# A new order of steps and a new deal of PSUM banks in a one-core attention and MLP kernel

## The chip, the core and the metric

The kernel runs on one core of a Trainium2 chip. The metric is the time of one execution on the device in microseconds (us), as a median of runs; lower is better.

## What is computed

```python
# q, k, v: 8 x 8 x 576 x 64 (batch, heads, sequence, head size); w_in 512 x 2048; w_out 2048 x 512
q_s = softmax(q, axis=-1)                    # over the 64 elements of a head
k_s = softmax(k, axis=2)                     # over the 576 places of the sequence
kv  = einsum('bhsd,bhse->bhde', k_s, v)      # 64 x 64 for each head
x   = einsum('bhsd,bhde->bhse', q_s, kv)     # back to 4608 tokens x 512
h   = x @ w_in
g   = h * tanh(softplus(h))                  # Mish
out = g @ w_out
```

Everything is float32.

## The kernel before

**Arithmetic.** Each large float32 product is made from three TensorE passes over numbers split in a high and a low part: high by high, high by low, low by high. `w_hi`, `x_hi`, `x_mix_hi`, `g_mix_hi` make high parts with a copy on ScalarE (ACT), and `w_lo`, `x_lo`, `x_mix_lo`, `g_mix_lo` make low parts with a subtraction on VectorE (DVE) or GpSimd (POOL). One pass is a matmul of 128 x 512.

**Stages.** A first block of tokens goes through the plain path: `h_part` (hidden layer, bank `ph`, line 629) and `out_part` (output, bank `po`, line 670). The other blocks go in pairs, k = 0 to 3, through a scheme that replaces eight block products by seven. `first_product(k, n, p)` (steps A, line 823) is product p, of 7, for the hidden piece n; it adds six matmuls into a bank `px`, `py` or `pz`. Products 1, 6, 5 and 3 of one piece add into the same bank `px`, and between them `partial` (steps C, line 859, ACT) copies the sum so far out of the bank; `joined` (J, line 863, DVE) and `g_mish_quad` (N, line 867, ACT) finish the piece. Then `g_mix` (GX), `g_mix_hi` (GH, line 889) and `g_mix_lo` (GK) prepare the Mish results, and `second_product(k, f, p)` (steps BB, line 839) multiplies them into banks `qx`, `qy`, `qz`. Each A or BB is six matmuls.

**Attention.** Heads come in pairs `e`. K (`a_kexp`, line 473) and Q are exponentiated on ACT; sums, maxima and transposes run on DVE, subtraction and scaling of Q on POOL. `a_kv2` (line 573, banks `pkv`, `pt`) makes the 64 x 64 matrices, `a_x2` (line 538, banks `px`, `pt`) applies them. The steps of attention for later blocks stand between the products of earlier ones.

**Weights.** `w_whole`, `w_mix` and `w_mix_out` build the weights of the seven products and write them to DRAM (`ws`). From there `w_fetch(e)` (steps F, line 807) brings them back in tiles of 512 KB, issued by POOL. Each tile serves two products. There are six slots:

```python
RING = ["w0", "w1", "xa0", "xa1", "xa2", "xa3"]
...
tag = {2: "w14", 3: "w15"}.get(e, RING[(e - LEAD) % 6])
...
nc.gpsimd.dma_start(dst, src)
```

So POOL can issue fetch e only when TensorE has read fetch e - 6 for the last time, and POOL takes its instructions one after another.

**Order.** The table `ORDER` lists 2,522 steps by name and number, and each engine's queue holds its instructions in that order. SyncE (SP) issues the other transfers in the same order: loads of K, Q and V, raw weights, stores of mixed weights and results. A second table, `BANKS`, gives one of TensorE's eight accumulation banks, a letter from a to h, to each of 282 uses, in the order in which they are asked for. A use waits until the use before it in the same bank has been read out. A planner outside the kernel wrote both tables; it isn't part of the program.

Of the kernel before, what the change touches and what calls it, by code (L numbers as in the profile page):

```python
# [9 lines left out]
F32 = mybir.dt.float32  # L10
# [27 lines left out]
Y10 RM27 ZT5 ZT4 RA27 G10 GL10 RB27 MQ7 RC27 SQ6 WM8.0p WM8.1p SQ7 WH8.0 RH26 Y9 GA9 WH8.1 RH27 RH25 H44 H45 H46 B6
H47 H48 WL8.1 WL8.0 KS6 GL9 RD22 WW9v R29 R28 LK8 ST5 WK1 WK10 WP8.0 WP8.1 WK3 WK9 RO25 RL28 RO26 WM9.0p WM9.1p RO27
Y11 GA11 RA28 EQ6 EK6 EQ7 RA29 RM29 MK8 GL11 RB28 RC28 RB29 Q6 QZ6 Q7 O8 H49 O9 H50 H51 H52 H56 H57 H53 H54 H55 H58  # L40
H59 O10 RH28 WH9.0 Y12 WH9.1 QZ7 WL9.0 RC29 WL9.1 WK11 WP9.0 WP9.1 RW30 KB8 RH29 GA12 Y13 GA13 Y14 GA14 KM8 WW10v GL12
GL13 GL14 QM7 RO28 QM6 WM10.0p WM10.1p KP6 XP4 UE8.0 RW31 WH10.0 WH10.1 S6 U8.0 O11 T7 O12 WL10.0 WL10.1 RB30 RC30
RB31 RC31 V8 WK4 WP10.0 WP10.1 LQ8 TC7 Z5 Z4 RH30 RD29 ZL5 ZL4 WW11v RD30 MQ8 T6 WM11.0p TC6 UE8.1 OP13.3 OP13.0 XP6
XT6 WM11.1p Z6 ZT7 Z7 ZT6 WH11.0 MS8 WH11.1 U8.1 ZL6 WL11.0 ZL7 WL11.1 MT8 SQ8 EQ8 LK10 WP11.0 ST7 WP11.1 LQ9 ST4 ST6
Q8 WW12v OP14.3 OP13.2 OP13.1 H60 H61 OP14.2 PK6 OP14.1 HM23 H62 H63 QW8 Y15 GM23 QV8 S8 MK10 MQ9 WM12.0p WM12.1p QM8
WH12.0 MS9 RH31 WH12.1 KB10 G15 GL15 WL12.0 MT9 KM10 WL12.1 T8 RO31 SQ9 UE10.1 EQ9 UE10.0 V10 WP12.0 WP12.1 LQ10 WW13v
Q9 QW9 U10.0 QV9 U10.1 MQ10 WM13.0p QM9 WM13.1p HM19 HM24 OP14.0 HM28 HM20 OP15.2 OP15.3 OP15.0 OP15.1 PA WH13.0 GM28
GM24 GM20 WH13.1 MS10 T9 WL13.0 EV0.0v WL13.1 WW14v MT10 PX8 PK8 SQ10 EV0.1s ZT9 Z8 ZT8 EQ10 LK12 WP13.0 WP13.1 LQ11
EV0.2v ZL8 S10 Q10 MK12 WM14.0p WM14.1p EV0.3s QW10 WH14.0 KB12 Z9 WH14.1 KM12 WL14.0 QV10 WL14.1 MQ11 UE12.1 MS11
QM10 V12 WP14.0 WP14.1 WK8 ST9 WW15v ZL9 MT11 T10 SQ11 EQ11 UE12.0 Q11 U12.0 U12.1 QW11 QV11 WM15.0p WM15.1p QM11 HM31  # L50
HM17 HM26 HM16 HM22 HM30 HM18 GM26 WH15.0 GM22 WH15.1 GM16 GM17 GM30 GM31 GH0.1.0 GM18 WL15.0 T11 WL15.1 WW0v LQ12
LK14 ST8 WP15.0 WP15.1 PX10 PK10 HM21 GM19 Z10 ZT10 Z11 WM0.0p MK14 ZL10 ZL11 MQ12 WM0.1p MS12 WH0.0 GH0.1.1 WH0.1
GM21 WL0.0 WL0.1 WW1v MT12 HM35 HM32 HM41 HM33 HM37 ST10 WK12 WP0.0 WP0.1 WK13 SQ12 WM1.0p WM1.1p ZT11 EQ12 WH1.0 GM37
GM32 GM33 WH1.1 KB14 GK0.1.1 WL1.0 WW6v Q12 WL1.1 S12 LQ13 WK14 WP1.0 WK6 WP1.1 WK15 WK7 MQ13 KM14 F4 WM6.0p WM6.1p
# [36 lines left out]
A1.7.3 BB1.3.1 PK22 PX22 BB1.4.1 BB1.5.1 A1.7.4 BB1.6.1 BB1.7.1 N1.6.2 N1.7.1 QW24 GH1.2.0 N1.3.2 GH1.2.1 GX1.3.0v
# [968 lines left out]
```

## Time and profile before

| | us |
|---|---|
| median of the runs | 788.44 |
| lowest of the runs | 788.32 |
| the profiled execution's own time | 787.31 |
| its span from first to last instruction | 785.5 |
| TensorE (PE) busy in the span | 773.4 |
| DVE, ACT, POOL busy | 560.6, 516.7, 298.3 |

The profiled execution's time is 1.8 us over its span, which is what lies before the first and behind the last instruction, and 1.1 us under the median. TensorE's granted clock is full in every stretch of the page. A matmul's listed duration, 0.39 us, holds its way through the pipeline, so consecutive ones overlap; their pace is read from their number in a stretch.

### The profile page before, as it was taken

The page shows a single profiled execution, that of the slowest core. Times are in us where ns is not written, and L with a number is a line of the kernel's source. Part 1 is how long each engine was busy: PE and PEld are TensorE (multiplying, and loading weights), DVE is VectorE, ACT ScalarE, POOL GpSimd, SP SyncE. Part 2 cuts the span into 40 slices and gives each one's busy share as a digit, 9 for nine tenths or more (in the row PEclk, how much of TensorE's full clock was granted, in tenths as well). Part 3 has the DMA queues.
Part 4 walks back from the last instruction along what each step waited for, and adds up shares of the span by engine and source line. Part 5 has one row for each costly group of instructions (what it writes and reads, how often), then busy time and mean ns, then how long its engine had stood idle before and what let it go on. Part 6 is the DMA issues. An engine that isn't in the chain of part 4 may idle for free.

```text
span 785.5 us, 12653 instructions
## 1 busy us (share of the span) xinstructions
PE 773.4 (98%) x4592; PEld 623.5 (79%) x4592; DVE 560.6 (71%) x877; ACT 516.7 (66%) x958; POOL 298.3 (38%) x378
## 2 busy tenths in 40 slices
PE   8999999999999999899999999999999999999997
PEld 7787768788877877687786878888878888888886
DVE  7999987765899999445799996235878722427863
ACT  7997867777887675588986765567736423635451
POOL 7898735544463444332332323133211121121111
PEclk9999999999999999999999999999999999999999
DMA  9996955678988878975775877668656684666575
GB/s 344 405 349 226 349 183 187 238 258 284 315 274 296 274 225 299 308 243 176 260 250 170 273 268 239 207 184 261 217 172 224 197 289 141 214 210 191 188 240 188
DMA packets 80717, 192.75 MB, mean 245 GB/s; under 512 B 16016, under 2 KB 28560, under 8 KB 80656
## 3 DMA queue, kind: packets, MB, share of 16 engines
q0 software_dynamic: 28800, 104.08, 41.5%
q1 hardware_dynamic: 51712, 87.74, 32.2%
q8 instruction: 36, 0.59, 0.3%
q14 instruction: 25, 0.20, 0.1%
q10 hardware_dynamic: 144, 0.13, 0.1%
HBM read 152.08 MB, written 39.85 MB: 244 GB/s over the span
## 4 chain that ended last, share of the span: by engine, by line
PE 75%; DVE 9%; ACT 8%; DMA 3%; issue 3%; POOL 1%; SPq 0%; DVEq 0%; ACTq 0%; POOLq 0%
PE qx L839 15%; PE px L823 14%; PE ph L629 10%; PE qz L839 10%; PE qy L839 9%; PE py L823 7%; PE pz L823 3%; PE px L538 2%; PE po L670 1%; PE pt L573 1%; DMA ws<-ws 1%; DVE gs L224 1%; DVE g L224 1%; DVE wa L269 1%; DVE w_out L726 1%
## 5 line engine op out<-in xcount | busy, mean ns | idle before, releaser
L807 POOL DMA_DIRECT2D ws<-ws x200 | 107.9, 542 | 348.7 <-PE qx L839 75.2
L224 DVE TENSOR_TENSOR gs<-g,gs 128x1024 fp32r<-128x1024 f32 x112 | 136.4, 1232 | 47.0 <-ACT gs L889 46.9
L889 ACT CAST gs<-g 128x1024 fp32r<-128x1024 f32 x112 | 116.5, 1051 | 76.2 <-PE qx L839 34.7
L839 PE MATMUL qx<-gs,ws 128*128 128x512 f32 x576 | 135.6, 391 | 0.0
L823 PE MATMUL px<-xh,ws 128*128 128x512 f32 x384 | 129.0, 391 | 2.3 <-DMA ws<-ws 2.0
L839 PEld LDWEIGHTS qx<-gs,ws 128*128 128x128 f32 x576 | 107.6, 188 | 26.3 <-issue 2.4
L629 PE MATMUL ph<-xs,wi 128*128 128x512 f32 x384 | 91.3, 392 | 0.6 <-DVE wc_out L276 0.5
L839 PE MATMUL qy<-gs,ws 128*128 128x512 f32 x384 | 90.9, 390 | 1.0 <-DVE gs L224 0.8
L839 PE MATMUL qz<-gs,ws 128*128 128x512 f32 x384 | 90.5, 390 | 0.0
L859 ACT COPY g<-px 128x512 f32<-128x512 f32 x72 | 41.5, 586 | 71.5 <-PE px L823 71.3
L823 PEld LDWEIGHTS px<-xh,ws 128*128 128x128 f32 x384 | 72.1, 188 | 19.3 <-issue 3.2
L839 PEld LDWEIGHTS qy<-gs,ws 128*128 128x128 f32 x384 | 71.8, 188 | 17.1 <-DVE gs L224 2.1
L629 PEld LDWEIGHTS ph<-xs,wi 128*128 128x128 f32 x384 | 71.4, 188 | 17.6 <-issue 2.0
L839 PEld LDWEIGHTS qz<-gs,ws 128*128 128x128 f32 x384 | 71.9, 188 | 16.5 <-issue 1.6
L224 DVE TENSOR_TENSOR g<-g,g 128x1024 f32<-128x1024 f32 x64 | 79.3, 1260 | 0.6
L823 PE MATMUL px<-xl,ws 128*128 128x512 f32 x192 | 74.7, 389 | 0.0
L863 DVE TENSOR_TENSOR g<-py,g 128x512 f32<-128x512 f32 x48 | 32.4, 683 | 57.7 <-PE py L823 29.6
L823 PE MATMUL py<-xh,ws 128*128 128x512 f32 x192 | 65.7, 390 | 0.0
L224 POOL TENSOR_TENSOR q<-q,qm 128x576 f32<-128x576 f32 (+1 forms) x31 | 41.2, 1328 | 31.9 <-DVE qm L383 18.6
L867 ACT ACTIVATE g<-g 128x512 f32<-128x512 f32 x72 | 43.2, 629 | 8.6 <-DVE g L863 8.3
L496 POOL TENSOR_TENSOR qe<-qe,qs 128x576 f32<-128x576 f32 x24 | 30.6, 1274 | 42.5 <-DVE qs L492 22.2
L629 PE MATMUL ph<-xs_odd,wi 128*128 128x512 f32 x192 | 44.9, 391 | 0.0
(169 smaller groups left out, 1287.9 us busy)
## 6 DMA issues: line engine op xcount, KB each, us to landing
ws<-ws POOLq DMA_DIRECT2D x197, 512.0 KB, 4.6
v<-in_v_dram SPq DMA_DIRECT2D x14, 594.0 KB, 5.8
ws<-m_out SPq DMA_DIRECT2D x32, 256.0 KB, 3.7
ws<-m_in SPq DMA_DIRECT2D x32, 256.0 KB, 3.5
raw_out<-in_w_dram SPq DMA_DIRECT2D x14, 512.0 KB, 7.7
kt_two<-in_kp_dram SPq DMA_DIRECT2D x12, 576.0 KB, 5.3
q<-in_qs_dram SPq DMA_DIRECT2D x24, 288.0 KB, 3.8
ws<-wi SPq DMA_DIRECT2D x24, 256.0 KB, 4.7
```

The lines of the kernel that those rows point to most:

```text
L224: eng.tensor_tensor(out, a, b, ALU.subtract)
L269: nc.vector.scalar_tensor_tensor(a, a, 3, low, ALU.logical_shift_left, ALU.bitwise_or)
L496: eng.tensor_tensor(q2, q2, z.unsqueeze(2).to_broadcast(list(q2.shape)), ALU.mult)
L538: nc.tensor.matmul((px, pt)[x][h][o], kvt[a, j], at[e + j]["qT"][x][a], start=True, stop=True)
L629: nc.tensor.matmul(gs[n], wi[f][:, a, t], x[:, z], start=t == 0 and i == 0, stop=t == HP - 1 and i == 2)
L807: nc.gpsimd.dma_start(dst, src)
L823: nc.tensor.matmul(dst, w[:, a, j], xc[k, p][z][:, j].rearrange("p b s -> p (b s)"), start=p in (1, 2, 7) and j == 0 and i == 0, stop=j == ...
L839: nc.tensor.matmul(psb[key, k][m], w[:, a, m], g[z][:, f % 2], start=first and i == 0, stop=f == NH - 1 and i == 2, skip_group_check=p in ...
L859: nc.scalar.copy(g_quad(k, n)[q], psb[1, k, n])
L863: nc.vector.tensor_tensor(g, psb[2 if q == 0 else 7, k, n], g, ALU.add)
L867: nc.scalar.activation(g, psb[1, k, n] if q == 1 else g, AF.Mish)
L889: nc.scalar.copy(t[0], gq[k, h][G_PART[p]])
```

## The change

The two tables are written anew by the planner. `ORDER` keeps its first 300 steps and holds the same 2,522 steps behind them in another sequence; `BANKS` keeps its first 70 letters. No function changes. The planner made the tables with two other settings: where POOL and DVE would take the port that they share at nearly the same moment, POOL is planned first; and a transfer is planned at 320 KB per us. No step changes its engine. Neither setting is in the program, which sees the order alone.

```diff
-RB16 RA18 RO14 RC16 RB15 RC15 H29 RH17 RA19 RM21 RH16 RH15 RA21 H30 H31 O5 RO17 RO16 RB19 RB18 RC19 RB21 RC18 RC21
...
+RB16 RA18 RO14 WK0 RB15 RM20 R31 RB18 RH17 RC16 RM21 QZ5 H29 RA19 RO17 RC15 H30 RH16 RB19 R26 RH15 H31 RC19 QM4 O5
...
 BANKS = """
...
-cfbhgebfdcefbgdh caefdfcebgbhcedb ghfdeacgbhgceaae aedfdfbaehfdabcg aefhfgbcbehdbagh dfcabgecfdhdecaf faafbggbfahbecdh
-gfcagbegdfehcdge fabfgchaedahahbf gdcechfgabdecfhe fbgeadbfhg
...
+hcgdfagdchbgeach gbedfaheahcgabdc ahebdhgfedacbfca bfhgbfdhgbfeddch adcecgfhcbadebea cgdhcdfbeaabghfe fefdceacbdeadbhg
+aefbdfgddhedbcfb dcfedcghabhbagef cdgbheagcfcfhbah eghefcdbhe
```

In the built program the number of matmuls, transfers and instructions of DVE and POOL is the same; ACT has 40 table loads in place of 46, because the order groups its functions differently. The engines leave the old order at about 57 us of the profiled execution (ACT and DVE), 59 us (POOL) and 67 us (PE).

**Place 1, the K and V product of pair 6** (`pkv6`, two banks; `po0` is the first block's output). On PE it follows one output step before:

```order
L670 MATMUL po0_0_610<-wo10_1001,gh10_1114 128x512 x2
L670 MATMUL po0_0_610<-wo10_1001,gl10_1116 128x512
L670 MATMUL po0_1_611<-wo10_1001,gh10_1114 128x512 x2
L670 MATMUL po0_1_611<-wo10_1001,gl10_1116 128x512
L670 MATMUL po0_2_612<-wo10_1001,gh10_1114 128x512 x2
L670 MATMUL po0_2_612<-wo10_1001,gl10_1116 128x512
L670 MATMUL po0_3_613<-wo10_1001,gh10_1114 128x512 x2
L670 MATMUL po0_3_613<-wo10_1001,gl10_1116 128x512
L573 MATMUL pkv6_1353<-v3_113,k6_1029 64x66
L573 MATMUL pkv6_1_1354<-v3_113,k6_1029 64x66
```

On DVE, the rows that end with the reading of bank `ph12`, which the second bank of `pkv6` takes over, were before (`gl` is a low part, `w_out` a whole weight):

```order
L726 TENSOR_TENSOR w_out2_1335<-wo2_668 128x512
L726 TENSOR_TENSOR w_out2_1335<-wo10_1001 128x512
L224 TENSOR_TENSOR gl12_1338<-ph12_1156,gh12_1326 128x512
L224 TENSOR_TENSOR gl13_1340<-ph13_1260,gh13_1329 128x512
L224 TENSOR_TENSOR gl14_1342<-ph14_1264,gh14_1332 128x512
```

On PE it now stands here, behind two groups of transposes (`pq6`, `pq7`) and another output step:

```order
L670 MATMUL po0_0_610<-wo12_1213,gh12_1265 128x512 x2
L670 MATMUL po0_0_610<-wo12_1213,gl12_1274 128x512
L670 MATMUL po0_1_611<-wo12_1213,gh12_1265 128x512 x2
L670 MATMUL po0_1_611<-wo12_1213,gl12_1274 128x512
L670 MATMUL po0_2_612<-wo12_1213,gh12_1265 128x512 x2
L670 MATMUL po0_2_612<-wo12_1213,gl12_1274 128x512
L670 MATMUL po0_3_613<-wo12_1213,gh12_1265 128x512 x2
L670 MATMUL po0_3_613<-wo12_1213,gl12_1274 128x512
L515 MATMUL pq7_1408<-ident_81,q7_1057 128x128 x4
L516 MATMUL pqt7_1409<-ident_81,q7_1057 128x128
L573 MATMUL pkv6_1415<-v3_113,k6_1090 64x66
L573 MATMUL pkv6_1_1416<-v3_113,k6_1090 64x66
```

On ACT, the rows from the end of the product `px4`, `px5` (just ahead of `pq6`) to the exponential `k6` that `pkv6` needs are now:

```order
L615 CAST xs_odd_1392<-px5_1358 128x512
L615 CAST xs_odd_1392<-px4_1357 128x512
L529 COPY qT6_1398<-pq6_1369 128x512
L530 COPY qTt6_1399<-pqt6_1370 128x64
L473 ACTIVATE k6_1090<-k6_1090 128x1152
```

The product moved behind later work, and its second bank is now one that `px5` had, no longer `ph12`.

**Place 2, fetch 170 of the weights** (k = 3; it takes the slot of fetch 164). On PE the twelve rows that end with its first reader were before, none of them reading `ws164`, whose last reader stands 21 rows above the first of them:

```order
L839 MATMUL qx3_0_7141<-gs3_1_0_6991,ws168_7065 128x512 x3
L839 MATMUL qx3_1_7142<-gs3_1_0_6991,ws168_7065 128x512 x3
L839 MATMUL qx3_0_7141<-gs3_1_0_6991,ws168_7065 128x512 x3
L839 MATMUL qx3_1_7142<-gs3_1_0_6991,ws168_7065 128x512 x3
L823 MATMUL px3_6_6951<-xh3_3_6524,ws167_7061 128x512
L823 MATMUL px3_6_6951<-xl3_3_6525,ws167_7061 128x512
L823 MATMUL px3_6_6951<-xh3_3_6524,ws167_7061 128x512 x2
L823 MATMUL px3_6_6951<-xl3_3_6525,ws167_7061 128x512
L823 MATMUL px3_6_6951<-xh3_3_6524,ws167_7061 128x512
L839 MATMUL qx3_0_7141<-gs3_1_1_6986,ws169_7063 128x512 x3
L839 MATMUL qx3_1_7142<-gs3_1_1_6986,ws169_7063 128x512 x3
L839 MATMUL qx3_0_7141<-gs3_1_1_6986,ws170_7129 128x512 x3
```

Now the row just ahead of the first of these is the last that reads `ws164`:

```order
L839 MATMUL qx3_0_7149<-gs3_1_0_7018,ws168_7097 128x512 x3
L839 MATMUL qx3_1_7150<-gs3_1_0_7018,ws168_7097 128x512 x3
L839 MATMUL qx3_0_7149<-gs3_1_0_7018,ws168_7097 128x512 x3
L839 MATMUL qx3_1_7150<-gs3_1_0_7018,ws168_7097 128x512 x3
L839 MATMUL qx3_0_7149<-gs3_1_1_6938,ws169_7078 128x512 x3
L839 MATMUL qx3_1_7150<-gs3_1_1_6938,ws169_7078 128x512 x3
L823 MATMUL py3_7_7112<-xh3_4_6645,ws171_7069 128x512
L823 MATMUL py3_7_7112<-xl3_4_6646,ws171_7069 128x512
L823 MATMUL py3_7_7112<-xh3_4_6645,ws171_7069 128x512 x2
L823 MATMUL py3_7_7112<-xl3_4_6646,ws171_7069 128x512
L823 MATMUL py3_7_7112<-xh3_4_6645,ws171_7069 128x512
L839 MATMUL qx3_0_7149<-gs3_1_1_6938,ws170_7158 128x512 x3
```

Between the last reader of the slot's old tile and the first reader of the new one stood 48 matmuls, and now 24. The same count for the 199 fetches that a matmul waits for, from the last matmul for which POOL must wait before it can issue the fetch (the reader of its own slot, or of one that stands ahead of it in POOL's queue) to the first that reads it: before, the smallest number was 30, eight times, and 26 fetches had 36; now three have 24, two 26 or 27, twelve 30, three about 32, and nineteen 36.

**Place 3, the bank `px3_0`** (k = 3, piece 0; `xh3_5` and `xh3_3` are the inputs of products 5 and 3). On PE the rows that end with the first matmul of product 3 were before, with product 5 further up:

```order
L823 MATMUL px3_1_6644<-xh3_5_6454,ws148_6688 128x512
L823 MATMUL py3_2_6754<-xh3_7_6513,ws148_6688 128x512
L823 MATMUL py3_2_6754<-xl3_7_6514,ws148_6688 128x512
L823 MATMUL py3_2_6754<-xh3_7_6513,ws148_6688 128x512 x2
L823 MATMUL py3_2_6754<-xl3_7_6514,ws148_6688 128x512
L823 MATMUL py3_2_6754<-xh3_7_6513,ws148_6688 128x512
L823 MATMUL py3_0_6613<-xh3_4_6734,ws146_6686 128x512
L823 MATMUL py3_0_6613<-xl3_4_6735,ws146_6686 128x512
L823 MATMUL py3_0_6613<-xh3_4_6734,ws146_6686 128x512 x2
L823 MATMUL py3_0_6613<-xl3_4_6735,ws146_6686 128x512
L823 MATMUL py3_0_6613<-xh3_4_6734,ws146_6686 128x512
L823 MATMUL px3_0_6584<-xh3_3_6524,ws146_6686 128x512
```

Now the first row is the last of product 5:

```order
L823 MATMUL px3_0_6624<-xh3_5_6512,ws144_6612 128x512
L823 MATMUL py3_2_6726<-xh3_7_6531,ws148_6679 128x512
L823 MATMUL py3_2_6726<-xl3_7_6532,ws148_6679 128x512
L823 MATMUL py3_2_6726<-xh3_7_6531,ws148_6679 128x512 x2
L823 MATMUL py3_2_6726<-xl3_7_6532,ws148_6679 128x512
L823 MATMUL py3_2_6726<-xh3_7_6531,ws148_6679 128x512
L823 MATMUL px3_0_6624<-xh3_3_6368,ws146_6681 128x512
```

One other product, six matmuls, now stands between the two that add into `px3_0`, where five stood before; the copy on ACT (line 859) has to fit in. In all, the places where a copy of line 859 or a Mish of line 867 has one product for it go from 11 to 24 between the start of k = 1 and the end, and two copies of line 767 join them.

## Rows read from the trace of the kernel before

**Rows 1.** The page: span, and busy time with share and instructions.

```profile
span 785.5 us, 12653 instructions
PE 773.4 (98%) x4592; PEld 623.5 (79%) x4592; DVE 560.6 (71%) x877; ACT 516.7 (66%) x958; POOL 298.3 (38%) x378
```

**Rows 2.** Windows, PE: length, busy us (instructions), granted clock, DMA share, GB/s.

```profile
55.00:140.00 85.00, 82.62 (x581) 1.00 0.71 238
140.00:300.00 160.00, 160.00 (x1123) 1.00 0.83 275
300.00:430.00 130.00, 126.45 (x702) 1.00 0.73 240
430.00:785.50 355.50, 351.54 (x1785) 1.00 0.68 216
```

**Rows 3.** Waits of PE: us in total, times, longest.

```profile
PE px L823 <- DMA ws<-ws: 2.0, 2, 1.3
...
PE pkv L573 <- DVE gl L224: 1.2, 1, 1.2
...
PE qy L839 <- DVE gs L224: 0.8, 1, 0.8
...
PE px L823 <- ACT g L859: 0.3, 1, 0.3
```

**Rows 4.** Windows, all engines (PE, PEld, DVE, ACT, POOL), one undisturbed stretch.

```profile
480.00:500.00 20.00, 20.00 (x90) 16.57 (x89) 7.38 (x17) 13.65 (x22) 6.09 (x9) 1.00 0.79 243
```

**Rows 5.** Line 807, the fetches: durations ns; time from issue to landing.

```profile
L807 POOL DMA_DIRECT2D ws<-ws x200: 527/535/753, 177.5 to 772.4; - x100
...
DMA to landing us min/median/max: 3.4/4.6/9.9
```

**Rows 6.** Timeline of POOL, 306 to 322 us: start, us, instruction.

```profile
314.59 0.57 POOL L807 DMA_DIRECT2D ws<-ws  x1
...
317.87 1.10 POOL L807 DMA_DIRECT2D ws<-ws  x2 [1.51 <-PE px L823]
```

**Rows 7.** Timeline of PE, 320 to 330 us.

```profile
322.22 0.47 PE L823 MATMUL px<-xh,ws 128*128 128x512 f32 x1 [0.66 <-DMA ws<-ws]
...
327.92 0.47 PE L823 MATMUL px<-xh,ws 128*128 128x512 f32 x1 [1.33 <-DMA ws<-ws]
```

**Rows 8.** Line 859, the copy out of a shared bank: ns min/median/max.

```profile
L859 ACT COPY g<-px x72: 565/589/631, 302.1 to 706.1; 128x512 f32<-128x512 f32 x72
```

**Rows 9.** Timeline of DVE, 97 to 103 us.

```profile
97.85 2.35 DVE L726 TENSOR_TENSOR w_out<-wo 128x512 f32<-128x512 f32 x2
100.12 1.87 DVE L224 TENSOR_TENSOR gl<-ph,gh 128x512 fp32r<-128x512 f32 x3
102.17 0.22 DVE L586 TENSOR_SCALAR rs<-pkv 128x1 f32<-128x1 f32 x2 [0.18 <-PE pkv L573]
```

**Rows 10.** Line 726, whole weights: ns min/median/max.

```profile
L726 DVE TENSOR_TENSOR w_out<-wo x16: 645/685/1784, 76.5 to 150.0; 128x512 f32<-128x512 f32 x16
```

**Rows 11.** ACT groups by line: count, busy us, mean ns, idle before.

```profile
L470 ACT ACT_TABLE_LOAD x12 | 15.4, 1283 | 2.9 <-DVE odd L510 2.2 <-DVE qTt L510 0.6
...
L529 ACT COPY qT<-pq 128x512 f32<-128x512 f32 x6 | 3.5, 589 | 3.1 <-PE pq L515 3.1
...
L473 ACT ACTIVATE k<-k 128x1152 f32<-128x1152 f32 x2 | 2.3, 1162 | 0.0
L615 ACT CAST xs_odd<-px 128x512 fp32r<-128x512 f32 x4 | 2.3, 592 | 1.8 <-PE px L538 1.0 <-DVE wc_out L276 0.8
...
L530 ACT COPY qTt<-pqt 128x64 f32<-128x64 f32 x4 | 0.9, 221 | 0.0
```

**Rows 12.** Timeline of PE, 104 to 112 us: transposes and an output step.

```profile
105.96 0.60 PE L515 MATMUL pq<-ident,q 128*128 128x128 f32 x4
...
106.42 0.70 PE L670 MATMUL po<-wo,gh 128*128 128x512 f32 x2
...
109.28 0.60 PE L515 MATMUL pq<-ident,q 128*128 128x128 f32 x4
```

More of the change, by code (lines that the diff above doesn't have):

```diff
@@ L38 @@
[L38 to L42, printed above, removed]
@@ new lines @@
+Q23 A1.7.5 GX1.1.1v F60 QW23 F58 QV23 A1.6.3 C1.7.3 MK26 BB1.0.1 MQ24 N1.0.3 J1.7.3 MS24 BB1.1.1 J1.4.2 N1.7.3
+GX1.0.1v N1.0.2 BB1.2.1 F62 GH1.2.0 QM23 A1.6.4 N1.6.1 N1.7.0 T23 N1.6.0 BB1.3.1 GX1.2.0v F61 GH1.1.3 J1.5.2 N1.6.3
+A1.7.3 MT24 GK1.1.3 PX22 N1.7.1 F64 F63 PK22 SQ24 BB1.4.1 GX1.3.0v EQ24 ZT23 KB26 LQ25 GK1.2.0 ST23 BB1.5.1 GH1.2.1
+V26 S24 XR23 BB1.6.1 J1.6.2 GK1.2.1 BB1.0.2 F66 N1.6.2 KM26 N1.4.2 MQ25 N1.5.2 A1.7.4 Q24 GX1.3.1v QW24 BB1.1.2 F65
+GH1.2.2 QV24 J1.7.2 QM24 BB1.7.1 N1.4.3 MS25 GK1.2.2 BB1.2.2 N1.7.2 GH1.2.3 MT25 GX1.2.1v BB1.3.2 GH1.7.0 F68 GK1.2.3
@@ new lines @@
+F67 BB1.4.2 GH1.7.1 GK1.7.0 BB1.5.2 F69 GX1.0.2v UE26.1 BB1.6.2 T24 DP1.0.0 GK1.7.1 GH1.7.2 BB1.0.7 F70 GX1.1.2v
+BB1.1.7 GX1.0.3v BB1.2.7 GH1.6.0 DP1.0.1 GK1.6.0 BB1.7.2 F72 GK1.7.2 BB1.3.7 GH1.7.3 F71 SQ25 DJ1.0.0 XR22 BB1.0.6
+DJ1.0.1 EQ25 GK1.7.3 DS1.0.1 GH1.6.1 BB1.4.7 Q25 ZT22 ST22 GX1.2.2v QW25 BB1.1.6 F73 DS1.0.0 LQ26 UE26.0 GK1.6.1
+BB1.5.7 QV25 BB1.6.7 QM25 GH1.6.2 T25 BB1.7.7 F74 U26.0 GX1.3.2v BB1.2.6 F75 GK1.6.2 GH1.6.3 PX24 F76 MQ26 BB1.3.6
+GX1.2.3v MS26 BB1.4.6 GH1.5.0 MT26 GK1.6.3 XR24 BB1.5.6 U26.1 SQ26 XR25 F77 BB1.6.6 GH1.5.1 GH1.3.0 GK1.5.1 BB1.7.6
@@ new lines @@
+EQ29 LQ30 Q29 A2.3.1 C2.2.0 J2.1.2 J2.0.2 A2.2.6 C2.3.0 A2.2.2 N2.0.2 C2.2.2 A2.3.6 F97 N2.1.3 MQ30 N2.0.1 F99 U30.0
+F100 A2.4.1 U30.1 A2.2.5 C2.4.0 N2.0.0 A2.4.2 C2.2.3 J2.2.3 A2.2.3 N2.2.3 F104 C2.3.2 A2.3.2 N2.2.1 QW29 A2.2.4 MS30
+A2.4.7 J2.2.2 F103 F101 MT30 J2.3.0 N2.2.2 A2.3.5 N2.1.0 J2.2.0 GH2.1.0 A2.3.7 N2.3.0 F105 GK2.1.0 C2.3.3 N2.2.0
+A2.4.6 QV29 F102 GH2.1.1 QM29 A2.3.3 T29 A2.5.1 J2.3.3 F106 SQ30 A2.5.7 EQ30 C2.4.2 LQ31 A2.3.4 C2.5.0 ST26 ST27
+A2.5.6 J2.3.2 F107 Q30 A2.4.5 C2.5.2 F109 A2.5.2 C2.4.3 J2.4.3 A2.4.3 J2.5.0 N2.3.1 GK2.1.1 N2.5.0 A2.4.4 QW30
@@ new lines @@
+GX2.1.0v N2.0.3 A2.6.2 N2.3.3 J2.4.0 N2.4.0 A2.6.1 GH2.1.2 A2.5.5 C2.6.0 F111 F108 J2.6.0 F110 A2.6.6 J2.4.2 C2.5.3
+GK2.1.2 A2.5.3 C2.6.2 MQ31 J2.5.3 MS31 A2.6.5 F113 N2.1.1 MT31 N2.6.0 A2.7.2 GX2.0.0v N2.5.1 QV30 PX28 F115 QM30 PK28
+XR29 XR28 A2.7.1 T30 ZT29 ZT28 ST28 S30 A2.6.7 C2.7.0 C2.6.3 J2.7.0 A2.7.6 J2.6.3 F112 XR32 GX2.0.1v ST29 A2.6.4
+C2.7.2 N2.6.3 A2.5.4 J2.6.2 A2.7.7 F114 SQ31 A2.7.5 XR33 F116 EQ31 DS1.2.1 DS1.2.0 Q31 BB2.0.1 C2.7.3 J2.7.3 BB2.1.1
+N2.7.0 GH2.1.3 A2.7.4 QW31 BB2.2.1 J2.7.2 N2.3.2 QV31 A2.6.3 J2.5.2 A2.7.3 N2.6.1 F117 N2.1.2 F118 GH2.2.0 F119
@@ L154 @@
+GK3.3.1 BB3.3.5 F193 BB3.2.3 GH3.3.2 GK3.3.2 BB3.4.5 BB3.5.5 F194 BB3.6.5 GH3.3.3 GK3.3.3 BB3.7.5 F195 GX3.1.3v
+BB3.3.3 DP3.1.1 DJ3.3.1 BB3.4.3 GX3.0.3v DS3.3.1 GH3.4.0 BB3.5.3 F197 GH3.4.1 GK3.4.0 BB3.6.3 DP3.1.0 GK3.4.1 BB3.7.3
+F198 DJ3.3.0 BB3.0.4 GH3.4.3 DJ3.1.0 DJ3.1.1 DS3.1.0 GH3.4.2 DS3.3.0 BB3.1.4 F199 DS3.1.1 F196 GK3.4.2 BB3.2.4 GK3.4.3
+BB3.3.4 BM3.4.4.0 BM3.5.4.0 BM3.6.4.0 BM3.7.4.0 BM3.4.4.1 DJ3.2.0 BM3.5.4.1 DS3.2.0 BM3.6.4.1 BM3.7.4.1 DK3.2.1.0
+DK3.2.1.1 DT3.2.1.0 DT3.2.1.1
 """
```

210 lines of the change are left out of this document (95 added, 115 removed).

## Prediction

> **What bounds the kernel now.** I read the page first. TensorE is busy for 773.4 of 785.5 us and no other engine is over 71% [rows 1], at a full granted clock in every stretch [rows 2]. So the question isn't which engine is slow on average, but where TensorE stands still, and whether it ever works below its own pace. The pace comes from an undisturbed stretch: 90 matmuls in 20.00 us [rows 4], 0.222 us for each pass of 128 x 512. With the number of matmuls unchanged, all that an order can change is idle time. The windows put it in place [rows 2]: 85.00 - 82.62 = 2.4 us between 55 and 140 us, none between 140 and 300, 130.00 - 126.45 = 3.5 us between 300 and 430, and 355.50 - 351.54 = 4.0 us behind 430. These last 4.0 are the tail, after the last matmul: joining and storing the last piece, which no order of the middle takes away. Idle time ahead of 55 us lies in the first 300 steps, which stay. So 2.4 + 3.5 = **5.9 us** is everything that the new order can remove. That makes a floor: 788.44 - 5.9 = 782.5 us, 0.75% under the median. A gain over 2%, which is about what a measurement of this kernel can tell from no change, would need 15.8 us and isn't there to be had.
>
> The waits of TensorE say what the 5.9 us are [rows 3]: 2.0 us in two waits for weight fetches, 1.2 us in one wait for DVE ahead of `pkv`, 0.8 us for a split of the Mish result on DVE, 0.3 us for a copy on ACT, and smaller ones. I go through them by kind, and ask for each what the new order puts in its place. The sum is made on the profiled execution; its differences are added to the median, which is 1.1 us above that execution's own time.
>
> **Waits for weight fetches, 2.0 us now.** A fetch takes 3.4 us at best, 4.6 at the median and 9.9 at worst from issue to landing [rows 5]. The two waits show what a slow one does. The fetch issued at 314.59 [rows 6] was used at 322.22 [rows 7], 7.6 us later, and TensorE stood for 0.66 us; the second of the pair issued from 317.87 on [rows 6] held it for 1.33 us at 327.92 [rows 7]. In the order these two had 30 and 36 matmuls between release and use, which is 6.7 and 8.0 us at 0.222 us each. So with 30 matmuls a median fetch has some 1.5 us to spare, and only a slow one is felt. The new order spends part of that margin (place 2): three fetches have 24 matmuls, 5.3 us; two have 26 or 27, 5.9 us; twelve have 30. The median fetch still lands in time for 24, by about 0.4 us if some 0.3 us pass between release and issue, an estimate. I price by the rate of before. One of eight fetches with 30 matmuls was slow, for 0.66 us: 0.08 us each, so twelve cost 1.0. One of 26 with 36 cost 1.33: 0.05 each, so the 22 with 32 or 36 cost 1.1. For 24 matmuls the same slow fetch, 7.6 + 0.3 us, would cost 2.6 us, for 26 or 27 some 2.0; at one in eight that is 0.32 and 0.25 each, 1.5 for the five. Sum **3.6 us in place of 2.0**. The bounds are 0, if all land at the median, and some 29 us if all twenty fetches under 33 matmuls land as late as the slow one (third rival).
>
> A page's rule speaks against a loss here. The rows have a median of 4.6 us for 512 KB [rows 5]. The Trainium skill, "DMA: Bandwidth & Descriptors", section on the anatomy of a DMA on the GpSimd path, has a fit of about 2.0 us plus the bytes over 436 GB/s, which by my working is 3.2 us for such a tile, below the fastest of the 200 rows; by it no fetch of either order would be late.
>
> **The pair-6 product, 1.2 us now.** Before, its second bank came from `ph12`, which DVE read late: two whole-weight additions took 2.35 us from 97.85, and the three low parts only began at 100.12 [rows 9]. In the new order (place 1) it needs the copies behind `px5` on ACT: two `xs_odd` at 592 ns, `qT` 589, `qTt` 221 and the exponential 1162 [rows 11], together 3.2 us. TensorE meanwhile has ten transposes and one output step: from 105.96 to 106.42 for five transposes, 106.42 to 109.28 for twelve passes [rows 12], 0.46 + 2.86 + 0.46 = 3.8 us. That covers the chain by 0.6 us, less handovers. I take 0.3 us, with bounds of 0 and 1.2. What is queued behind the waiting `pkv6` is all of TensorE. Its result then feeds `pt6` after one group of six matmuls, 1.3 us, through five small DVE instructions that stand behind a `w_out`. That addition takes 685 ns at the median and 1784 at most [rows 10]; I take 0.2 us more, with bounds of 0 and 1.5. The other 1.2 us of idle time between 55 and 140 us I leave as they are, with bounds of 0 and 3: this stretch keeps its crowd of weight conversions in another order, and I see no reason for either sign. So **2.4 becomes 1.7**.
>
> **Copies out of a shared bank, 0.3 us now.** Where product 5 and product 3 of a piece have one product between them (place 3), the copy of 589 ns [rows 8] must fit into six matmuls, 1.3 us. It does if ACT is free, with 0.7 us over; it fails if ACT is in a cast or a table load, 1283 ns [rows 11]. Before there were 11 such places, and one cost 0.3 us: 0.025 each. Now there are 26: **0.6 us**, from 0 to 5 if a table load stands in front of several.
>
> **The rest.** The waits for splits and the single small ones, 1.3 us, are kept at 1.3 (0 to 3): the chain from the last first products over Mish and splits to the second products has the same steps. Six table loads fewer, 6 x 1.283 = 7.7 us less on ACT [rows 11], are worth nothing on the path: ACT is idle for a third of the span [rows 1], and TensorE, which sets the end, hides it. SP and POOL hold the same transfers. POOL's Q steps now stand at other places between fetches, and since a fetch behind them waits, that is in the counts of place 2 only where a matmul is behind it.
>
> **Sum.** 3.6 + 1.7 + 0.6 + 1.3 = 7.2 us of idle time in place of 5.9, so 1.3 more: 788.44 + 1.3 = **789.7 us**, no change that a measurement would tell.
>
> **Rivals.** First, *the fetches land in time and their waits vanish*: 789.7 - 3.6 = 786.1 us, down to the floor of 782.5 if the other waits go too. For it: 4.6 us at the median fits even 24 matmuls [rows 5]; against it: before, two fetches with more room were late. The skill's DMA page would have it so. Chance 0.22. Second, *DVE becomes the bound between 55 and 140 us*: whole-weight additions stretch from 0.69 to 1.78 us at worst [rows 10] while POOL works beside them. If five or six more are stretched by 1.1 us, or an equal delay comes from the new order, in a part where DVE has no slack, TensorE waits for about 6 us more: 796 us. Chance 0.08. Third, the slow side: *the fetches become the bound from k = 1 on*. POOL issues in its order, so TensorE waits for each late tile. The price of a mean landing T on the twenty short ones is 20 T - 123.5 us: 3 (T + 0.3 - 5.3) and so on for each group. At the slow fetch's 7.6 us that is 29 us, 27 more than before: 815 us. It decides from about T = 7.1 us, where it takes 18 us; the median of 4.6 speaks against it, the 9.9 us of the worst for it. Chance 0.05. That the new order leaves TensorE's waits as they were gives 788.4 and falls under the forecast.
>
> **How the numbers follow.** The forecast has the remaining 0.65, spread over some 786 to 794 us. The range should leave out no more than 2 in 10: at its low end I take the floor, 782.5, since nothing below it can be had; at the high end the forecast with about half of the upper bounds (fetches 9, early part 4, copies 2, rest 2, 17 in all against 5.9) gives 799, and I stop at 798, so that the third rival is outside. Faster by over 2%: 0.01, a TensorE that ran faster than its own pace. Slower by over 2%: 0.05, the third rival. Within 2%: 0.94.
>
> **What would show it.** TensorE's busy time again near 773 us and 90 matmuls in 20 us. The wait ahead of `pkv6` at most a few tenths, for ACT or DVE and no longer for `gl`. Waits for `ws` in more places than two, mainly where k = 1 and 2 read the tiles with 24 matmuls, each under 2.6 us. The copies of line 859 named more than once. I'm wrong if idle time between 140 and 300 us, which is none now, appears, or if TensorE's idle time behind 55 us, tail apart, is over 16 us or under 2.

## The result, and the profile after

The changed kernel takes **781.8 us** at the median of its runs (781.06 to 782.77), against 788.76 for the kernel before: a ratio of 0.9914, with a 95% interval of 0.9895 to 0.9934. One of the four runs of before took 961.67 us; the ratio leaves it out, and without it the median of before is 788.44. The changed kernel is 0.9% faster, less than the 2% that I called the bound of a change, but clearly not none, and on the other side of 788.44 than my 789.7. It lies 0.7 us below the range's low end, which I had called a floor.

The page of the profiled execution after (its own time 782.30 us), which answers to [rows 1]:

```profile
span 780.5 us, 12662 instructions
...
PE 770.3 (99%) x4592; PEld 623.5 (80%) x4592; DVE 563.7 (72%) x877; ACT 511.0 (65%) x952; POOL 297.3 (38%) x378
```

The span is 5.0 us shorter. TensorE's *busy* time is 3.1 us shorter too, with the same 4592 instructions at a full granted clock. That was not on my list of things that an order can change. The windows after, beside [rows 2] (length, busy us with instructions, granted clock, DMA share, GB/s):

```profile
core 0: us, PE busy (x), PEclk, DMA share, GB/s
0.00:55.00 55.00, 52.50 (x420) 1.00 0.98 370
55.00:140.00 85.00, 84.63 (x612) 1.00 0.80 264
140.00:300.00 160.00, 159.08 (x1087) 1.00 0.82 262
300.00:430.00 130.00, 129.17 (x797) 1.00 0.82 254
430.00:780.50 350.50, 344.95 (x1688) 1.00 0.68 214
```

Idle time between 55 and 140 us went from 2.38 to 0.37 us, between 300 and 430 us from 3.55 to 0.83. Between 140 and 300 us, where there was none, 0.92 us came, and behind 430 us, where only the tail stood idle (4.0 us), it is 5.6 us now: a tail of 4.1 and 1.5 us of waits. The waits of TensorE behind 55 us, beside [rows 3] (us in total, times, longest):

```profile
engine line waited for: us in total, times, longest us
PE pz L823 <- DMA ws<-ws: 1.2, 1, 1.2
PE qz L839 <- DVE gs L224: 0.7, 1, 0.7
PE px L823 <- ACT g L859: 0.5, 2, 0.3
PE pkv L573 <- ACT k L473: 0.3, 1, 0.3
PE px L823 <- DMA ws<-ws: 0.3, 1, 0.3
PE qx L839 <- DVE gs L224: 0.2, 1, 0.2
PE qy L839 <- DMA ws<-ws: 0.2, 1, 0.2
```

With one more of 0.09 us, too short for this view, the waits there sum to 3.6 us, where 5.9 stood before and I had forecast 7.2.

**Where time hides inside busy time.** To see the rest I count *starts*: the time at which the n-th matmul of a full array with 512 columns starts, n from 0 to 3119. Both kernels run 3,120 of these, so the difference of the two times at the same n is what one is ahead, whatever the list calls idle. The stretches are cut so that each holds the same number of all other matmuls in before and in after. This table, worked out so from the traces, gives for each stretch how much longer (+) or shorter (-) it is than in the profiled execution of before. The stretches are named by their times in before: n = 0 at 20.3 us, 500 at 153, 966 at 267, 1300 at 351, 2268 at 588, and the last takes in the tail. "First 20" is the part ahead of n = 0, the same steps in all. Labels are those of the experiments below; e9_after is the changed kernel again, e4_mru its order with a poor deal of banks.

```
              first 20  to 153  153-267  267-351  351-588  588-end   span
after           +0.58    -3.62    +1.20    -2.75    -1.26    +0.85   -5.00
e9_after        +0.44    -3.70    +4.09    -3.28    -1.59    +1.28   -2.77
e1_abb          +1.08    -3.59   +15.21    -0.77    -0.27    +0.59  +12.25
e2_bab          +0.85    -0.08    +7.05    -1.23    +0.57    +0.35   +7.52
e3_bba          +0.80    -0.08     0.00    +5.58    +0.45    +1.49   +8.24
e4_mru          +2.08    +1.85    +4.19    -2.14    -1.37    +2.23   +6.84
e5_ab500        +0.60    -3.66    +8.64    +0.22    -0.29    +0.69   +6.19
e6_aba          +0.49    -3.63   +10.15    -3.06    -0.86    +1.04   +4.12
e7_moves        +0.02    +1.90     0.00    -0.87    -0.09    +0.29   +1.25
e8_lru          +0.61    -3.64    +1.65    -2.92    -1.01    +1.57   -3.74
e10_best        +1.01    -3.65    +0.55    -3.01    -0.44    +0.87   -4.67
e11_lrub        +0.51    +1.86    +0.39    -0.18    -0.19    +0.10   +2.48
e12_abal        +0.53    -3.63   +11.85    -3.13    -1.95    +1.42   +5.08
e13_ab966       +1.02    -3.71    +1.05    +3.71    -0.39    +0.83   +2.50
e14_ba966       +0.22    -0.19     0.00    -2.43    -1.01    +1.57   -1.84
e15_px24        +0.78    -0.16     0.00    +0.21    -0.62    +0.55   +0.75
```

The gain lies mainly at two places: 3.6 us up to 153 us, and some 3 us between 267 and 351 us. Between them 1.2 us are given back, and 351 to 588 us brings 1.3 us more. Single numbers need care: in the order of before, the stretch from 267 to 351 us varies from -0.87 (e7) to +0.22 (e5), and that from 351 to 588 us from -0.39 (e13) to +0.57 (e2). In the last column but one all kernels with the order of before there (e1, e2, e5, e7, e11, e13, e15) show +0.10 to +0.83, so the profiled execution of before was lucky there by about 0.5 us, and after loses little. The first 20 us differ by chance as well, the steps being the same in all (and the banks, e4_mru aside, in nearly all). Without these two, after is about 6.1 us ahead (5.00 + 0.58 + 0.5), nearer to the 7.0 us between the medians.

Up to 153 us listed idle time fell by 2.0 us, starts by 3.6: 1.6 us had been inside what the list calls busy. The list does two things here. It shows a wait too short, as here (timeline of PE, before):

```profile
88.83 2.38 PE L629 MATMUL ph<-xs,wi 128*128 128x512 f32 x9
91.66 5.04 PE L629 MATMUL ph<-xs,wi 128*128 128x512 f32 x21 [0.45 <-DVE wc_out L276]
```

The last of the nine starts at 90.81 us and the next matmul 0.85 us later, where 0.22 is the pace; of the 0.63 us lost the list shows 0.45 as idle. And some waits it doesn't show at all. How the 1.6 us divide between the two is not worked out. A place later in the kernel shows the second kind. The timeline of before, the product of the attention step of pair 24 on PE and on its weight loads (PEld):

```profile
425.09 0.19 PEld L538 LDWEIGHTS px<-qT,kvt 64*64 64x64 f32 x4 [0.35 <-issue]
425.09 2.10 PE L538 MATMUL px<-qT,kvt 64*64 64x512 f32 x8
425.36 0.70 DVE L509 STREAM_TRANSPOSE qT<-qe 128x512 f32<-128x512 f32 x1
...
426.12 0.19 PEld L538 LDWEIGHTS px<-qT,kvt 64*64 64x64 f32 x4 [0.83 <-DVE qT L509]
```

PE's row says 2.10 us of busy time for eight matmuls, with no idle time ahead. But the weight loads of the second four stood 0.83 us for the transposed queries of the odd item, which DVE wrote until 425.36 + 0.70 = 426.06 us. From the first start to the next row's start this visit, as I call such a group between other work, took 2.03 us. In after the same eight take 1.02. These matmuls list at least 0.59 us each, longer than the way from one start to the next in an undisturbed visit, so a wait between two of them closes up in the sum. Only the start times, or PEld's own waits, show it.

### The profile page after: what moved, and what is told of

The parts are those of the page before. It is cut to its first block, busy times and chain, and to the rows that moved or that the text cites. A ratio compares the mean times of both kernels' runs of the same rounds, so it can differ in the third digit from the quotient of the medians.

```text
span 780.5 us, 12662 instructions
## 1 busy us (share of the span) xinstructions
PE 770.3 (99%) x4592; PEld 623.5 (80%) x4592; DVE 563.7 (72%) x877; ACT 511.0 (65%) x952; POOL 297.3 (38%) x378
## 4 chain that ended last, share of the span: by engine, by line
PE 68%; DVE 9%; ACT 7%; DMA 7%; issue 4%; POOL 3%; SPq 1%; DVEq 0%; POOLq 0%; ACTq 0%
PE px L823 15%; PE qx L839 14%; PE qy L839 8%; PE qz L839 8%; PE py L823 7%; PE ph L629 6%; PE pz L823 4%; DMA ws<-ws 2%; PE po L670 2%; DMA q<-in_qs_dram 2%; DVE gs L224 2%; PE px L538 1%; DMA ws<-m_in 1%; PE pt L573 1%; POOL m_in L739 1%
## 5 line engine op out<-in xcount | busy, mean ns | idle before, releaser
L839 PE MATMUL qz<-gs,ws 128*128 128x512 f32 x384 | 92.2, 391 | 0.7 <-DVE gs L224 0.7
L629 PEld LDWEIGHTS ph<-xs_odd,wi 128*128 128x128 f32 x192 | 35.8, 188 | 8.3 <-issue 0.8
```

The source lines that it names most:

```text
L629: nc.tensor.matmul(gs[n], wi[f][:, a, t], x[:, z], start=t == 0 and i == 0, stop=t == HP - 1 and i == 2)
L839: nc.tensor.matmul(psb[key, k][m], w[:, a, m], g[z][:, f % 2], start=first and i == 0, stop=f == NH - 1 and i == 2, skip_group_check=p in ...
```

## The experiments

Three theories stand against each other. **Places**: the gain is a set of waits at single places, part of them inside busy time; each stretch has its own and they add up. **Even gain**: better banks or fewer table loads make every stretch a little shorter. **Deal**: the banks carry it, and not the order of steps. All times below are medians, ratios are against before in the same group of runs, with 95% intervals.

### Both orders in one kernel

Each takes the first steps of one order and then the rest in the sequence of the other; banks follow the order in use as far as live ones allow. Steps around the seam of e5_ab500, the point at which one order takes over from the other, where `-` is the order of after and `+` what follows instead, that of before without the steps already done:

```diff
 EQ11 GH0.1.1 LQ12 Q11 WP13.1 HM30
-KM12 WW14v UE12.1 WK7 QW11 ZT8 QV11 UE12.0 HM24 QM11 ST8 U12.0 T11 WM14.0p
+WK3 WK4 HM24 GM24 WW14v ZT8 WM14.0p WM14.1p WH14.0 WH14.1 KM12 WL14.0 WL14.1 UE12.1
...
```

> The order and deal of after for its first 743 steps (to about 165 us), then the remaining steps in the order of before, with the deal of before as far as the banks that are live at the seam allow. Place theory (the gain is a handful of waits that are gone at their places, and adds up by stretch): matmul by matmul the profiles of before and after part by 3.6 us between 60 and 155 us, so about 785 us, -3.6 against before (788.6). Rival, an even gain (other banks or fewer table loads make every stretch a little shorter): 105 of 720 us of matmuls, so -1.0, 787.6. Rival, the gain lies behind 300 us where the fetches are: 0.

> The order of before to about 165 us, that of after to about 333 us, and that of before again. Place theory: between these two points the two profiles part by 2.0 us more (the two waits for fetched weights at 322 and 328 us go, a wait for a split at 230 us comes), so -2.0, 786.6. Even gain: -1.6, which this run can't tell from it. If the waits for fetches come back with the late order of before around the seam, 0.

> The order of before to about 333 us, and that of after from there. Place theory: behind 333 us the two profiles part by only 0.1 us (the hidden wait of an attention visit at 425 us and split visits go, -1.5, a wait of 1.2 for a fetch at 465 us and other small ones come), so 0 to -1, 788. Even gain: 450 of 720 us lie there, so -4.2, 784.4.

> The order of after for its first 500 matmuls of 512 columns (to 150 us) and that of before from there, with a seam at which no bank is asked for within 12 steps of its last use. Place theory: the stretch that ends at 150 us is 3.6 us shorter in after, and the rest stays as in before, so -3.6 (785.0), with the trace the same as that of before behind the seam to 0.3 us. Even gain: 130 of 720 us, -0.9 (787.7).

Measured: e1_abb 797.9 us (1.0124, 1.0109 to 1.0140), e2_bab 793.6 (1.0066, 1.0054 to 1.0078), e3_bba 795.1 (1.0086, 1.0070 to 1.0102), e5_ab500 794.0 (1.0066, 1.0053 to 1.0078). All slower than both parents, and no theory expected that. As times these four miss. e1_abb, e2_bab and e3_bba lose 15.2, 7.1 and 5.6 us in the stretch that holds their first or only seam. By stretch e5_ab500 says more: ahead of the seam it is shorter by 3.66 us where after is by 3.62, and behind it, from 267 to 588 us, it is in step with before to 0.3. All that it loses is one place, the first attention product behind the seam (timeline of PE):

```profile
162.91 2.97 PE L538 MATMUL px<-qT,kvt 64*64 64x512 f32 x6 [6.16 <-ACT g L646]
```

The windows around it in the same kernel show a second cost:

```profile
150.00:156.70 6.70, 6.70 (x30) 1.00 0.96 346
156.70:160.00 3.30, 0.05 (x1) 0.86 0.87 323
160.00:162.90 2.90, 0.00 (x0) 0.50 0.49 134
162.90:166.00 3.10, 3.09 (x14) 0.51 0.56 198
166.00:168.00 2.00, 2.00 (x78) 1.00 0.91 335
```

TensorE's granted clock is full ahead of the wait, falls to its lower level (0.50) while it stands still, stays there for the first 3.1 us of work (0.51) and is full again from 166. The 6.2 us of waiting so became 8.6 us.

Between the seam and that product the mix has two blocks of the hidden layer for TensorE, as after has (`HM24`, `HM17`), but all of the mixing of weights 14 and 15 (steps `WM` to `WP`), of which after has only the beginning there. The chain of work that ends with the product (145 to 163.5 us) is for 36% stores of mixed weights landing (`ws<-m_out`) and for 21% their mixing on POOL (`m_out`). Whether the bank or these steps came last there, a plain deal of banks tells:

> The order of after to 150 us, that of before to 266 us, and that of after again. In the middle after is 1.2 us longer than before (two waits for splits at 230 and 258 us), and from 266 us 3.2 us shorter. Place theory: -3.6 - 3.2 = -6.8 against before by the profiles (781.8), 1.2 us less than after has itself, if the seam at 266 us costs nothing; each wait that comes there is paid in full. Even gain: (130 + 515) of 720 us of the gain of after, so 782.5, slower than after.

> The order of e6_aba (after to 150 us, before to 266, after again) with all banks dealt by the plain rule. If the 6.2 us that TensorE waits behind the first seam of e6_aba are a bank that was asked for too soon: the seam goes and the sum of the stretches shows, 781 to 783. If they come from ScalarE, which has the steps of both orders to do around a seam: 790 to 792 as e6_aba.

e6_aba 792.1 us (1.0038, 1.0025 to 1.0052), e12_abal 792.7 (1.0054, 1.0039 to 1.0070). With 207 of 282 letters changed the wait stays (6.76 us at 164.47, now put down to the transposed queries on DVE), which speaks for the steps ahead of the product and against the bank. And again the stretches hold: up to 153 us both have -3.63, from 267 to 351 us -3.06 and -3.13, about as after has (-2.75).

The cleanest seam is at 266 us, where the two orders have done the same steps but for eight:

```diff
 F23 DP0.2.0 EQ17 DP0.2.1 ST14 LQ18
-LK20 V18 BB0.1.3 BB0.0.5 BB0.1.5 Q17 GK0.5.1 WW5v BB0.2.5 WH4.1 GH0.5.2 GH0.5.3 GK0.5.2 MQ18
+GX0.1.3v BB0.0.5 Q17 LK20 V18 ZT15 QW17 GK0.5.1 ST15 BB0.1.3 QV17 BB0.1.5 GH0.5.2 QM17
...
```

These are the steps of e14_ba966 (before, then after); e13_ab966 is the mirror image.

> The order of after to 266 us (966 matmuls of 512 columns), where the two orders have done the same steps but for 8, then that of before; no bank had to change at the seam. Place theory: the first part of after is 2.4 us shorter by the profiles (3.6 gained to 150 us, 1.2 given back at 230 and 258 us), the second is that of before: 786.2 if the seam is clean. Rival, that the gain lies in the order as a whole or behind 266 us: 788.6.

> The order of before to 266 us and that of after from there. Place theory: -3.2 by the profiles, and about 1.1 us back for the wait that e6_aba had at this seam (273 us): 786.5, with the trace in step with that of after behind the seam to 0.5 us. Rival: 788.6.

e14_ba966 takes **785.6 us** (0.9967, 0.9956 to 0.9979), expected 786.5: with only 0.4 us lost at the seam, the part behind 266 us alone gives 2.6 us of time. e13_ab966 takes 791.7 (1.0045, 1.0031 to 1.0059), slower than both of its forecasts. Its stretches ahead of the seam are those of after (-3.71, +1.05), but behind it three splits are late (timeline of PE):

```profile
271.12 2.83 PE L839 MATMUL qx<-gs,ws 128*128 128x512 f32 x11 [1.73 <-DVE gs L224]
274.61 0.50 PE L839 MATMUL qx<-gs,ws 128*128 128x512 f32 x1 [0.66 <-ACT gs L889]
275.87 1.43 PE L839 MATMUL qx<-gs,ws 128*128 128x512 f32 x5 [0.76 <-DVE gs L224]
```

So the early gain of 3.6 us is shown in nine traces of eight kernels, to 0.1 us, but as time only inside after. The even gain falls with these runs: two stretches of after carry 6.4 of the 7.6 us that it gains, and one is longer than before. Fewer table loads can't be the reason either, by the same traces: up to 153 us after has 13 of them where before has 11, and from 267 to 351 us both have 5. The six fewer lie between 351 and 588 us (12 for 18), where after gains 1.3 us; from 153 to 267 us, where it loses 1.2, it has 10 for 12.

### The deal of banks alone

The order of after with two other deals, and the order of before with the plain one. The first 60 letters in after, in e4_mru and in e8_lru:

```diff
-abcdefghadbcefgahebcfbagehdgabcgehfdabchfbeahcfbhgdeaefcacae
+aabcabcabcdeadeadbabdcaefghfdfhgdfbhfadafabdffbdhgaebfebcbfc
...
-abcdefghadbcefgahebcfbagehdgabcgehfdabchfbeahcfbhgdeaefcacae
+abcdefghadbcgefahgbceafbghdabfcghaedbfcaefhbacefagdhbhecbcbh
```

> The order of after, with every PSUM bank dealt as badly as the order allows: each request takes, of the free banks, the one that was given up last. If the order alone carries the gain and banks are given up early enough in it: 782 to 784. If the deal carries it: the waits for evacuations come back behind each request, some 210 behind the first 70, and if only one in ten costs 0.3 us, +6 us, 788 or above.

> The order of after with the PSUM banks dealt by one plain rule: each request takes, of the free banks, the one that was given up longest ago, in the order of the steps. If the deal of the change matters only in that it keeps away from banks that were just given up: 781 to 783, as after. If the deal is fitted to this order beyond that: 785 or above.

> The order of before with the PSUM banks dealt by the plain rule of e8_lru (of the free banks the one given up longest ago). If the order carries the gain: 787.5 to 790, as before. If the deal of before was the poorer part: 783 to 786.

e4_mru 797.0 us (1.0117, 1.0097 to 1.0137), e8_lru 782.6 (0.9923, 0.9909 to 0.9936), e11_lrub 791.6 (1.0042, 1.0027 to 1.0056). A bad deal costs 15 us; the plain rule, with 167 letters other than the change has, costs the new order nothing that can be measured. On the old order the plain rule is 3 us worse than its own deal, more than either forecast had; one wait stands out (timeline of PE):

```profile
126.10 1.21 PE L629 MATMUL ph<-xs_odd,wi 128*128 128x512 f32 x4 [2.63 <-ACT g L646]
```

With the same plain rule on both, the new order is about 9 us faster than the old one. So the change's deal is not what makes it faster: the order is, and the rival that names the deal falls. But the order needs a deal that keeps off banks just given up: with e4_mru's the early gain is gone (+1.85 up to 153 us), while that from 267 to 351 us mostly stays (-2.14).

### Single waits taken away

```diff
-KP6 XP4 UE8.0 RW31 WH10.0 WH10.1 S6 U8.0 O11 T7
+XP4 UE8.0 RW31 WH10.0 WH10.1 U8.0 OP11.0 KP6 S6 OP11.1 OP11.2 OP11.3 T7
...
-PX24 ... XR25 XR24 ... BB1.2.6 BB1.3.6 BB1.4.6 PK24
+... BB1.2.6 BB1.3.6 PX24 XR25 XR24 BB1.4.6 PK24
```

> The kernel of before with two steps moved: the keys-by-values product of pair 6 behind the first quarter of the second product's block 11, and the attention step of pair 24 behind two more blocks of the second product, each with the copies that follow it. Place theory: the wait of 1.17 us of the first (99.35 us) and the wait of about 1.0 us of the second that lies within its matmuls' busy time (425 us, 2.03 us in place of 1.02) both go, some 0.2 comes back as one more change between kinds of matmuls: -2.0 (786.6), of which only 1.2 were to be seen as idle time of PE. If only idle time counts: -1.0 (787.5). If the waits come up again at the next step: 0.

791.2 us (1.0035, 1.0023 to 1.0048): slower, the third case and worse. The timeline of PE:

```profile
101.47 1.68 PE L538 MATMUL px<-qT,kvt 64*64 64x512 f32 x8 [2.02 <-DVE gl L224]
...
428.85 1.09 PE L538 MATMUL px<-qT,kvt 64*64 64x512 f32 x8
...
432.16 0.32 PE L538 MATMUL pt<-qTt,kvt 64*64 64x64 f32 x2 [0.63 <-ACT raw L767]
432.64 0.27 PE L538 MATMUL pt<-qTt,kvt 64*64 64x64 f32 x1 [0.16 <-ACT raw L767]
```

With the pair-6 product out of the way, `px4` and `px5` stood first, and they wait for a low part that DVE writes later still, through the bank that `px5` takes over: 2.02 us in place of 1.17. At pair 24 the hidden wait is gone (the visit at 428.85 takes 1.02 us from start to start), but its tail must have the same two banks, the only ones not held by sums, and waits 0.8 us for the copies out of them. Hence one more, where the tail is moved as well:

```diff
-PX24 ... XR25 XR24 ... BB1.2.6 BB1.3.6 BB1.4.6 PK24 BB1.5.6
+... BB1.2.6 BB1.3.6 PX24 XR25 XR24 BB1.4.6 BB1.5.6 PK24
```

> The kernel of before with the attention step of pair 24 moved alone: its product behind two more blocks of the second product, the copies of its result behind it, and its tail (which uses the same two banks, the only free ones) behind two blocks more in place of one, so that the copies are done. If the wait inside the busy time at 425 us is real work time and e7_moves lost it to the tail's banks: the visit takes 1.02 in place of 2.03, the tail 1.33, and -1.0 shows behind 435 us: 787.6. If something else comes due there: 0.

787.9 us (0.9993, 0.9985 to 1.0002): no change. The timeline of PE:

```profile
428.60 1.09 PE L538 MATMUL px<-qT,kvt 64*64 64x512 f32 x8
...
434.84 0.96 PE L839 MATMUL qx<-gs,ws 128*128 128x512 f32 x3 [0.44 <-DVE gs L224]
```

The visit's 1.01 us and the tail's wait are gone, and now a split is late. In the table 351 to 588 us is 0.62 us shorter, 0.2 to 0.4 of it beyond what e5, e11 and e13 show there with the same steps. The hidden wait was real, and more than half of what it gives is asked back a few us later.

### On top of the change

> The changed kernel once more, beside the other runs of this group: 781 to 783.

> The changed kernel with two steps moved: the maximum over item 16's queries stands behind the split for product 2's second group (on VectorE, where it waits for its load and holds up that split), and the load of the values of pair 30 stands some 70 steps later (on SyncE, where it runs beside the fetch for which TensorE waits at 465 us). If each wait that shows in the trace is paid in full and nothing else is late within that distance: -0.7 to -0.9 for the first (the wait at 230.5 us, in part that at 258), -1.2 for the second, 779.8. If the next step is late too, as in e7_moves: 781 to 782, and the waits stand at other places. If the fetch lands late for other transfers than this load: -0.8 alone, 781.0.

The edit, against after:

```diff
-MQ16 GH0.2.1 GX0.2.1v BB0.7.1 GM29 F10 GH0.2.2 GK0.2.1
+GH0.2.1 GX0.2.1v BB0.7.1 GM29 F10 GH0.2.2 GK0.2.1 MQ16
...
-V30
...
 UE30.0
+V30
```

e9_after 782.0 us (0.9922, 0.9907 to 0.9938), e10_best 781.2 (0.9913, 0.9899 to 0.9928). The times of the two can't be told apart; the traces can. The wait at 230 us is a load that VectorE's queue passes on. In e9_after it was long (timeline of DVE, then of PE):

```profile
229.13 0.76 DVE L392 TENSOR_REDUCE qm<-q 128x18 f32<-128x576 f32 x1 [2.51 <-DMA q<-in_qs_dram]
229.80 1.22 DVE L224 TENSOR_TENSOR g<-g,g 128x1024 f32<-128x1024 f32 x1
230.93 1.22 DVE L224 TENSOR_TENSOR gs<-g,gs 128x1024 fp32r<-128x1024 f32 x1
```

```profile
232.21 0.96 PE L839 MATMUL qz<-gs,ws 128*128 128x512 f32 x3 [2.24 <-DVE gs L224]
```

The maximum waits 2.51 us for its queries, the split behind it ends at 232.15, and TensorE stands 2.24 us (0.69 in the first profile of after). With the maximum behind the split, e10_best has no wait there, and its stretch from 153 to 267 us is +0.55 in place of +1.20 and +4.09. The second step did nothing: at 465.52 us TensorE waited 1.89 us, now put down to low parts on DVE, where after had 1.19 for the fetch. The fetch landed within 0.1 us of their end, 9.2 us after its issue, against 8.5 in after. So the load that I moved was not what held it up; what does, stays open.

## Why the prediction failed, step by step

**The step that failed is the floor**: "5.9 us is everything that the new order can remove", with 782.5 us as a bound that nothing could pass. It took TensorE's listed idle time for its waiting time, and its busy time for fixed. Listed idle time behind 55 us fell by 2.3 us (5.9 to 3.6); 3.1 us more came out of busy time. On the two profiled executions alone, 5.0 us apart, the 5.9 would not have been passed; what breaks the floor is where the time came from. Waits at weight loads inside an attention visit (425 us above, 1.0 us) and the listed ends of matmuls (0.18 us at 90.81 us) had covered them. I had read the pace in one undisturbed stretch, 0.222 us [rows 4], and multiplied it with nothing. Counting starts over the whole trace shows it: the matmuls that are not 128 x 512 took 59.0 us in before from their starts to the next ones and take 55.8 in after, and only 1.4 of these 3.2 us are listed as idle.

Of the 7.9 us between 789.7 and 781.8, 3.6 are listed waits (7.2 forecast, 3.6 measured) and 3.1 are busy time, put at nothing. The rest is mostly that the profiled execution of before lies 1.1 us under its median and that of after 0.5 above its own. The sign of the change was missed through the listed waits: the fetches were priced 1.9 us too high and the stretch up to 140 us 1.3.

**Up to 140 us** I had 2.4 becoming 1.7 us; it became 0.37, and 1.6 us hidden in busy time up to 153 us went as well. The pair-6 product did what I said, 0.34 us for ACT's `k`, not for `gl` (0.3 forecast). The 0.2 us for its tail and the 1.2 us "as they are" are gone altogether. Keeping 1.2 us with bounds of 0 and 3, "no reason for either sign", was the larger part of the 1.3 us. In the new order the crowd of conversions meets TensorE nowhere else; which of the moved steps frees it the runs don't single out, since e7_moves shows that one step alone makes it worse.

**Fetches**: 3.6 us forecast, 1.7 measured (1.19, 0.28 and 0.22; in e9_after 2.1, as 1.43 and 0.64). The rate "one of eight" that I carried from 30 matmuls to 24 was wrong. The three fetches with 24 matmuls landed 3.93 to 4.03 us after issue, and the twelve with 30 in 3.5 to 5.2. Fetch 170 of place 2 has 24, is issued at 697.07 us and landed 4.03 us later (timeline of POOL, then of PE where it is read):

```profile
697.07 1.06 POOL L807 DMA_DIRECT2D ws<-ws  x2 [3.55 <-PE py L823]
```

```profile
701.72 0.39 PE L823 MATMUL py<-xh,ws 128*128 128x512 f32 x1
701.94 1.30 PE L839 MATMUL qx<-gs,ws 128*128 128x512 f32 x5
```

No wait. The late ones had 27, 32 and 36 matmuls and took 5.9, 8.5 and 7.9 us. So what made a fetch late was its landing, more than its room, and the rate taken from fetches with more room did not go over to those with less. Why these three took long isn't settled; e10_best took one load out of the way of the slowest, in vain. The landings are 3.4, 4.6 and 8.5 us at least, median and most, beside [rows 5]. The fit of the Trainium skill, "DMA: Bandwidth & Descriptors", 3.2 us for such a tile by my working, would have none late; three were, and no landing is as short, so the trace does not agree.

**Copies out of a shared bank**: 0.6 us forecast, 0.55 measured in two waits. Right, with some luck: in e9_after it is one wait of 0.28.

**The rest**: 1.3 us kept, about 1.0 measured (0.69 and 0.23 for splits at 230 and 258 us, 0.09). These came at new places, between 140 and 300 us, which I had named as a sign that I was wrong.

**Table loads at nothing**: no run singles out the six fewer, but the two stretches with the gain have two more and as many as before, so a price for them would not explain it.

**Rivals.** The first, waits for fetches that vanish, pointed the right way with 0.22 and had only a third of the reason: the two waits at 322 and 328 us went, most of the 3 us between 267 and 351 us, and others came. The second and third rival did not happen. No rival had the early stretch getting better.

## What to carry over

Before calling listed idle time of TensorE a floor, count starts: compare the time from first to next start of each kind of visit with the shortest one of its kind, and read the waits of the weight loads beside those of the matmuls. Waits at single places add up by stretch. The early gain, which hangs on engines, held from kernel to kernel to 0.1 us; a wait that hung on a load differed by 1.5 us between two executions. Taking one wait away by moving one step mostly showed the next step that is late (e7_moves, e15_px24); the order that gained had all steps around planned anew.

## What the runs showed of the hardware

Kernels with the same first steps and banks differ by up to 1.1 us in the first 20 us, and a wait that hangs on a load differed by 1.5 us between two executions of one program (0.69 and 2.24 us at the same matmul). The granted clock fell to its lower level, 0.50, in a wait of 6.2 us (e5_ab500) and was full again only after 3.1 us of work; in the kernels before and after the change, where no wait is over 1.4 us, it reads 1.00 in every window. A list of busy times can hold a wait of 1.0 us with no idle time beside it (425 us).
